# Linear attention and gated FFN on one core: reordering the first four units' state, mask, output and evacuation work

## The chip, the cores and the metric

One core of a Trainium2 chip. The metric is the device time of one execution in microseconds (us); lower is better.

## The reference, cut to what matters

```python
# q, k, v: [4, 8, 768, 64]; lam: [8]; blocks of 64 positions
for b in range(nb):
    intra = einsum('bhic,bhjc->bhij', qb, kb) * Dmask
    intra = einsum('bhij,bhjd->bhid', intra, vb)
    inter = einsum('bhid,bhde->bhie', qb * lam_pow, kv_state)
    out[:, :, sl] = intra + inter
    kv_state = lam_block * kv_state + einsum('bhsd,bhse->bhde', kb * rev_pow, vb)
x = out.transpose(0, 2, 1, 3).reshape(3072, 512)
return (x @ w_a) * (x @ w_b) @ w_out
```

Decayed linear attention, then a bilinear FFN on its 3072 rows.

## The kernel before

The kernel cuts the rows into 24 units of 128. Attention of a group of units is woven between the FFN products of the group before it. The first group, units 0 to 3, has nothing to hide behind: its attention runs first, and the FFN starts when its output `xT` is copied out of PSUM. The change edits only that start. For each unit *intra* multiplies masked scores with v, *inter* multiplies q with the state of the units before, and both add up in one PSUM tile `o`.

```python
def mask(kq, split=False):
    ...
        if split and i == 1:           # one mask of eight goes by ScalarE to GpSimd
            nc.scalar.copy(raw_kq, kq[i])
            nc.gpsimd.tensor_mul(m, raw_kq, lotri_bc)
        else:
            nc.vector.tensor_mul(m, kq[i], lotri_bc)

def inter(u):      # 4 products, full array: lhsT = state [128 x 128]
def intra(u):      # 8 products, lhsT = vb [128 x 64]: half the array's columns each

def kv_copy(u, ps, eng="dve"):         # state out of PSUM
    if eng == "act":                   # two copies of 64 x 256
    else:                              # one product of 128 x 512 with bdiag
    ...
def evac_o(u, xT, col, eng="act"):     # o[128 x 512] -> xT, by ScalarE or VectorE
    ...
    for u in range(n0):                # n0 = 4
        make_vb(u, "pool")             # v cast to bf16 on GpSimd
    ...
    scores4(1, (0, 1), ((5, 2), (6, 0)))
    for hps in ((0, 1), (2, 3)):
        for u in range(3):
            kv_part(u, hps)            # kv products: 2 * (u + 1) each time
            if hps[0]:
                kv_copy(u, sts[u], ("act", "act", "dve")[u])
    ...
    intra(0, True)
    evac_o(0, *xTs[0])
    intra(1, True)
    inter(1)
    evac_o(1, *xTs[1], eng="dve")
    intra(2, True)
    intra(3, True)
    inter(2)
    evac_o(2, *xTs[2], eng="dve")
    inter(3)
    evac_o(3, *xTs[3])
```

(`...` marks cuts. Unit 0 has no state before it, so no inter.)

## Time and profile before

| | before |
|---|---|
| median, first three runs | 233.85 us (233.6 to 234.01) |
| span of the profiled run, its time | 231.8 us, 233.49 us |
| TensorE busy | 97% of the span |
| first FFN product starts | 18.59 us |
| TensorE's last wait of note | 0.45 us, just before that product |

Read it this way: after 18.59 us TensorE waits for next to nothing, so the time is that start plus a constant. The lines are in the prediction.

### The profile page before, as it was taken

Reading aid. Unit: us, or ns where it says so; the run is one execution under the profiler, and the core shown is the slowest. Engines: PE = TensorE matmul, PEld = TensorE weight load, DVE = VectorE, ACT = ScalarE, POOL = GpSimd, SP = SyncE. Lnnn points to the kernel's source line nnn. Section 1 sums busy time; section 2 is a strip of 40 time slices with the busy share of each in tenths; the row PEclk is TensorE's granted clock in tenths of the full one; section 3 lists DMA queues with packets and bytes.
Section 4 is the critical chain, followed back from the end, with each engine's and each line's share of the span. In section 5 each row is a group of like instructions: output and inputs, shape, how many; then the busy total and the mean of one; then the engine's idle time right before and its main releaser. Section 6 shows DMA issues by size and latency. Waiting matters only on the chain.

```text
span 231.8 us, 4520 instructions
## 1 busy us (share of the span) xinstructions
PE 225.2 (97%) x1775; PEld 124.6 (54%) x1775; DVE 115.9 (50%) x204; ACT 91.1 (39%) x172; POOL 50.6 (22%) x65
## 2 busy tenths in 40 slices
PE   7799999999999999999999999999999999999994
PEld 2474444449698554454544454544454544444494
DVE  0896566636469726684334484235583323332050
ACT  3585754066463342333233332333332233332251
POOL 6070000248373333445000543001200000000000
PEclk9999999999999999999999999999999999999999
DMA  4999999999999999998759997229300220000311
GB/s 151 303 283 351 348 364 293 295 207 223 185 225 176 224 208 209 209 197 190 270 189 200 220 182 121 91 96 205 65 3 0 91 93 0 1 0 5 130 49 48
DMA packets 96389, 38.84 MB, mean 168 GB/s; under 512 B 83312, under 2 KB 91888, under 8 KB 96368
## 3 DMA queue, kind: packets, MB, share of 16 engines
q1 hardware_dynamic: 96224, 38.54, 72.9%
q8 instruction: 14, 0.23, 0.4%
q14 instruction: 7, 0.06, 0.1%
q10 hardware_dynamic: 144, 0.00, 0.0%
HBM read 28.32 MB, written 6.29 MB: 149 GB/s over the span
## 4 chain that ended last, share of the span: by engine, by line
PE 92%; DMA 3%; ACT 2%; SPq 1%; DVE 0%; issue 0%
PE a_ps L435 27%; PE b_ps L435 27%; PE op L467 27%; DMA k<-in_k_dram 3%; PE o_ps L352 3%; PE kq L310 2%; PE o_ps L342 2%; PE kvd L366 2%; PE tps L296 1%; ACT o_kept L458 1%; SPq L209 1%; PE kq L578 1%; ACT xT L359 0%; PE kv L366 0%; PE tk L542 0%; DVE scratch L531 0%
## 5 line engine op out<-in xcount | busy, mean ns | idle before, releaser
L447 DVE TENSOR_TENSOR ab<-a_sb,b_ps 128x512 bf16<-128x512 bf16 (+2 forms) x96 | 52.3, 552 | 77.9 <-PE b_ps L435 56.9
L435 PE MATMUL a_ps<-xT,wa_sb 128*128 128x512 bf16 (+2 forms) x384 | 77.2, 326 | 0.6 <-ACT xT L359 0.6
L435 PE MATMUL b_ps<-xT,wb_sb 128*128 128x512 bf16 (+2 forms) x384 | 77.2, 326 | 0.0
L442 ACT CAST a_sb<-a_ps 128x512 bf16<-128x512 f32 (+2 forms) x96 | 45.6, 481 | 63.1 <-PE a_ps L435 61.5
L467 PE MATMUL op<-wo_sb,ab 128*128 128x512 bf16 (+2 forms) x312 | 65.6, 363 | 0.0
L435 PEld LDWEIGHTS <-wb_sb 128*128 128x128 bf16 x384 | 34.5, 98 | 28.7
L435 PEld LDWEIGHTS <-wa_sb 128*128 128x128 bf16 x384 | 33.7, 98 | 29.1 <-POOL wa_sb L162 0.6
L467 PEld LDWEIGHTS <-ab 128*128 128x128 bf16 x312 | 28.8, 98 | 29.9
L327 DVE TENSOR_TENSOR m<-kq,lotri 128x512 bf16<-128x512 f32 x47 | 29.3, 682 | 18.1 <-PE kq L310 17.8
L259 POOL TENSOR_TENSOR qk<-kf,lp_k 128x512 bf16<-128x512 f32 x18 | 18.9, 1049 | 74.7 <-DMA kf<-in_k_dram 47.3
L264 POOL TENSOR_TENSOR qk<-qf,lp_q 128x512 bf16<-128x512 f32 x20 | 22.0, 1099 | 23.4 <-DMA qf<-in_q_dram 23.4
L462 ACT COPY o_sb<-op 128x512 f32<-128x512 f32 (+2 forms) x19 | 10.3, 541 | 34.0 <-PE op L467 34.0
L359 ACT CAST xT<-o_ps 128x512 bf16<-128x512 f32 x22 | 12.0, 590 | 17.9 <-PE o_ps L352 17.5
L398 DVE TENSOR_TENSOR st<-kvd,bdiag 128x512 bf16<-128x512 f32 x18 | 12.3, 682 | 4.9 <-PE kvd L366 3.8
L273 DVE CAST vb<-vf 128x512 bf16<-128x512 f32 x17 | 9.4, 553 | 0.0
L298 ACT COPY qkT<-tps 128x1024 bf16<-128x1024 bf16 x5 | 5.1, 1012 | 9.9 <-PE tps L296 9.9
L197 PE MATMUL idle<-idle_sb 128*128 128x128 bf16 (+1 forms) x31 | 7.2, 372 | 1.3 <-DVE idle_sb L192 1.3
L352 PE MATMUL o_ps<-m,vb 128*64 128x128 bf16 x192 | 7.9, 222 | 0.0
L273 POOL CAST vb<-vf 128x512 bf16<-128x512 f32 x7 | 4.7, 666 | 14.0 <-DMA vf<-in_v_dram 14.0
L342 PEld LDWEIGHTS <-st 128*128 128x128 bf16 x80 | 5.4, 98 | 2.8
L310 PE MATMUL kq<-qkT 64*128 64x128 bf16 x160 | 6.6, 218 | 0.0
L352 PEld LDWEIGHTS <-vb 128*64 128x64 bf16 x192 | 5.8, 109 | 1.4
(57 smaller groups left out, 87.4 us busy)
## 6 DMA issues: line engine op xcount, KB each, us to landing
vf<-in_v_dram SPq DMA_DIRECT2D x24, 256.0 KB, 4.9
qf<-in_q_dram SPq DMA_DIRECT2D x20, 256.0 KB, 4.4
kf<-in_k_dram SPq DMA_DIRECT2D x20, 256.0 KB, 4.6
out_dram<-o_sb SPq DMA_DIRECT2D x16, 256.0 KB, 2.0
wst<-in_moe_w_a_dram SPq DMA_DIRECT2D x6, 512.0 KB, 8.7
wst<-in_moe_w_b_dram SPq DMA_DIRECT2D x6, 512.0 KB, 8.8
wst<-in_moe_w_out_dram SPq DMA_DIRECT2D x6, 512.0 KB, 8.5
out_dram<-o_kept SPq DMA_DIRECT2D x7, 256.0 KB, 2.5
```

The costliest lines, as they stand in the source:

```text
L259: eng_of(eng).tensor_mul(qk[:, 1], raw.pop((u, "k")), lp_k[:, u % NB].to_broadcast([128, H, D]))
L264: eng_of(eng).tensor_mul(U[u]["qk"][:, 0], raw.pop((u, "q")), lp_q[:, u % NB].to_broadcast([128, H, D]))
L273: eng_of(eng).tensor_copy(vb, vf)
L310: nc.tensor.matmul(kq[i][:, hp, :], lhsT=d["kT"][p, hp, :], rhs=d["qT"][p, hp, :], start=True, stop=True, skip_group_check=True)
L327: nc.vector.tensor_mul(m, kq[i], lotri_bc)
L352: nc.tensor.matmul(d["o"][p, hp, :], lhsT=d["vb"][:, 2 * hp + i, :], rhs=d["m"](i, hp), start=(first and hp == 0), stop=True, skip_group_c ...
L359: nc.scalar.copy(xT[:, :, col:col + BLK], o_ps)
L398: nc.vector.tensor_mul(st[:].rearrange("p hp i d -> p hp (i d)"), ps[:].rearrange("p hp i d -> p hp (i d)"), bdiag_bc)
L435: nc.tensor.matmul(ps[:, :gt], lhsT=w_sb[:, s, f * 128:(f + 1) * 128], rhs=xT[:, s, :gt], start=(s == 0), stop=(s == KS - 1))
L442: nc.scalar.copy(a_sb[:, :gt], ps[:, :gt])
L447: nc.vector.tensor_mul(ab[:, f, :gt], a_sb[:, :gt], ps[:, :gt])
L467: nc.tensor.matmul(op[:, lo:hi], lhsT=ab[:, f, t * 128:(t + 1) * 128], rhs=wo_sb[:, f, lo:hi], start=(f == 0), stop=(f == FC - 1))
```

## The change

The intent: unit 0's and 1's states complete sooner, so that ScalarE is free sooner; GpSimd's mask no longer waits behind a v cast; ScalarE takes unit 2's evacuation while TensorE computes unit 3; and unit 3's, the last and exposed one, is shared by two engines. The whole diff:

```diff
-    for u in range(n0):
+    for u in range(n0 - 1):
         make_vb(u, "pool")
     ...
     scores4(1, (0, 1), ((5, 2), (6, 0)))
-    for hps in ((0, 1), (2, 3)):
-        for u in range(3):
-            kv_part(u, hps)
-            if hps[0]:
-                kv_copy(u, sts[u], ("act", "act", "dve")[u])
+    make_vb(3, "pool")
+    for u in range(2):
+        kv_part(u, (0, 1))
+    for u in range(2):
+        kv_part(u, (2, 3))
+        kv_copy(u, sts[u], "act")
+    kv_part(2, range(HP))
+    kv_copy(2, sts[2], "dve")
     ...
     intra(2, True)
+    inter(2)
+    evac_o(2, *xTs[2])
     intra(3, True)
-    inter(2)
-    evac_o(2, *xTs[2], eng="dve")
     inter(3)
-    evac_o(3, *xTs[3])
+    xT, col = xTs[3]
+    o3 = U[3].pop("o")
+    nc.scalar.copy(xT[:, 0:2, col:col + BLK], o3[:, 0:2])
+    nc.vector.tensor_copy(xT[:, 2:4, col:col + BLK], o3[:, 2:4])
```

## The prediction

> **What bounds the kernel now.** I read the page first, then the waits of TensorE, then the timeline of each engine from 14 to 19.5 us, where the edited lines run.
>
> From the page: the engines' busy time and the chain that ended last.
>
> ```profile
> PE 225.2 (97%) x1775; PEld 124.6 (54%) x1775; DVE 115.9 (50%) x204; ACT 91.1 (39%) x172; POOL 50.6 (22%) x65
> PE 92%; DMA 3%; ACT 2%; SPq 1%; DVE 0%; issue 0%
> ```
>
> TensorE is busy for 97% of the 231.8 us and is 92% of the chain. The next view lists all that TensorE ever waited for (total us, times, longest).
>
> ```profile
> PE idle L197 <- DVE idle_sb L192: 1.3, 1, 1.3
> PE tq L542 <- DVE scratch L531: 0.8, 4, 0.2
> PE tk L542 <- DVE scratch L531: 0.7, 2, 0.4
> PE a_ps L435 <- ACT xT L359: 0.6, 2, 0.5
> PE tn L562 <- ACT scratch L553: 0.2, 1, 0.2
> ```
>
> Only one of these is near the change: the first FFN product (L435) waits 0.45 us for the last evacuation of xT (L359). The remaining 0.1 us of that row is the only TensorE wait after it. So from the first FFN product on, TensorE runs its own stream with nothing to wait for, and the time of the kernel is the start of that product plus a constant. The whole question is: at what time does the first FFN product start, and can the three behind it follow it? In the kernel before it starts at 18.59 us. TensorE there:
>
> ```profile
> 14.19 0.67 PE L366 MATMUL kv<-vb,scratch 128*128 128x128 bf16 x6
> ...
> 15.36 0.50 PE L366 MATMUL kvd<-vb,scratch 128*128 128x128 bf16 x6
> 15.79 0.64 PE L352 MATMUL o_ps<-m,vb 128*64 128x128 bf16 x16
> 16.36 0.40 PE L342 MATMUL o_ps<-scratch,st 128*128 128x128 bf16 x4
> 16.69 0.68 PE L352 MATMUL o_ps<-m,vb 128*64 128x128 bf16 x16
> 17.30 0.62 PE L342 MATMUL o_ps<-scratch,st 128*128 128x128 bf16 x8
> 17.75 0.39 PE L562 MATMUL tn<-ident,scratch 128*128 128x128 bf16 x4
> 18.59 1.24 PE L435 MATMUL a_ps<-xT,wa_sb 128*128 128x512 bf16 x5 [0.45 <-ACT xT L359]
> ```
>
> L366 are the kv products, L352 intra, L342 inter. One row follows the other with no idle time marked. A product here lasts 0.22 us but the next is issued 0.056 us later (six products in 0.50 us: 0.22 + 5 x 0.056). So TensorE, not ScalarE, paces this stretch until 17.92 (17.30 + 0.62), the end of the last inter product. The other engines:
>
> ```profile
> 15.40 1.51 ACT L396 CAST st<-kv 64x256 bf16<-64x256 f32 x4 [0.50 <-PE kv L366]
> 16.94 0.59 ACT L359 CAST xT<-o_ps 128x512 bf16<-128x512 f32 x1
> 17.95 0.59 ACT L359 CAST xT<-o_ps 128x512 bf16<-128x512 f32 x1 [0.43 <-PE o_ps L342]
> 15.66 1.16 POOL L325 TENSOR_TENSOR m<-scratch,lotri 128x512 bf16<-128x512 bf16 x1
> 17.73 0.69 DVE L361 CAST xT<-o_ps 128x512 bf16<-128x512 f32 x1 [0.25 <-PE o_ps L342]
> ```
>
> ScalarE idled 0.43 us before unit 3's evacuation, waiting for TensorE. So the tail of the stage is: last inter product ends 17.92, +0.04, ScalarE copies for 0.59 to 18.54, +0.05, first FFN product at 18.59. GpSimd's mask ends at 16.82 (15.66 + 1.16), 0.13 after intra of unit 2 began at 16.69; that intra reads the mask in its sixth product, which by the 0.056 rhythm would have come at 16.83, and came at about 16.87. So the mask cost TensorE about 0.04 us.
>
> **What the Trainium skill says.** TensorEngine Tiling (Array Packing), section Key Properties: changing the tiling mode, not just the tile, drains TensorE. This trace agrees: intra is in mode 128*64, kv and inter in 128*128. The last of the 16 intra products is issued 0.22 before 16.43, at 16.21, and the next inter product at 16.36: 0.15 us. From inter to the transposes of L562, the same mode, it is 17.70 to 17.75, 0.056. A switch thus costs about 0.095 us more than going on.
>
> PSUM — Partial Sum Buffer, section PSUM bank collisions raise a hardware error: two engines may not access one bank in the same partitions at the same time, ScalarE and VectorE reading it included, and must be guarded by semaphores per bank and quadrant. No trace here shows a collision, but the built program shows the guard: in the changed kernel's order, VectorE's half copy of unit 3 waits for ScalarE's semaphore alone, at the count that ScalarE's half copy of the same bank reaches. So the two halves run one after the other, not side by side.
>
> **The change part by part.** I replay the stage with the rhythms above.
>
> 1. kv products of units 0 and 1 first. The 24 products stay 24, in one mode; they end at 15.86 as before. Unit 0's state is complete after 8 products rather than 14: six steps of 0.056 = 0.34 us earlier. ScalarE's four copies of L396 (1.51 us) move from 15.40–16.91 to about 15.06–16.57; it is free of its cast (L324) at 14.90, so nothing is in the way. Evacuation of unit 0 ends about 17.19 instead of 17.52. TensorE waited for none of them: inter of unit 1 came at 16.36, exactly one switch after intra, with its state ready at 16.14. Worth on the path: 0.
>
> 2. The mask ahead of unit 3's v cast. ScalarE's cast of the raw scores ends at 14.90, so GpSimd runs the mask at about 14.95–16.10 and the v cast (0.62) to 16.7. Both are there when wanted (16.69, and 17.36 for unit 3's intra). Removes the 0.04 us of TensorE's wait.
>
> 3. New order intra 2, inter 2, intra 3, inter 3, in place of intra 2, intra 3, inter 2, inter 3. This lets ScalarE evacuate unit 2 while unit 3 is computed, but adds two mode switches: 2 x 0.095 = 0.19 us, plus the first pair of products after a switch, which is 0.02 slower than a pair in stride. Replay: intra 2 16.69 to its last issue at 16.88; inter 2 issued 17.03–17.21, done 17.43; intra 3 17.36–17.55; inter 3 17.70–17.88, done 18.10. Before: 17.92. So the last inter product comes 0.18 us later. Evacuation of unit 2 on ScalarE runs 17.47–18.06, so ScalarE is just free for unit 3 at 18.14.
>
> 4. Unit 3 in halves. ScalarE's half, 128x256: its copies of 256 columns (L396) take 0.37 in place of 0.59, so it ends at 18.14 + 0.37 = 18.51. VectorE's half starts after that. Its duration is an estimate: VectorE's product L447 takes 686 ns at 512 columns and 416 at 256 by the groups by form, 0.27 less, so 691 - 270 = 420 ns; about 18.55–18.97.
>
> Start of the FFN: products read xT in four parts; parts 0 and 1 are ScalarE's half, 2 and 3 VectorE's. First product at 18.51 + 0.05 = 18.56 (before 18.59). Products follow each other at 0.215 us, so the third wants VectorE's half at 18.99 and gets it at 18.97 + 0.05 = 19.02; before it ran at 18.59 + 0.43 = 19.02. Sum: +0.18 (order) - 0.22 (shorter last copy) = -0.04 for the first product, and +0.03 of new wait in front of the third: about 0.00 us in all.
>
> After that: VectorE's cast of the first wb chunk slips from 18.34–19.02 to about 18.9–19.6; it is wanted at 20.1 or later. The next chunk's cast waits for its DMA till 20.79 in any case. Neither reaches the path.
>
> **The rivals.**
>
> A. The intent holds: unit 3's evacuation really halves, because VectorE and ScalarE are both free. For it: VectorE's last evacuation ends at 18.42 before. If the halves ran side by side, xT would be whole at 18.56 and the gain 0.03 us; the two extra drains eat the rest. If moreover the drains cost nothing, the last inter ends at 17.88 (0.04 for the mask), the first FFN product starts at 18.34, and the time falls by 0.25 us, to 233.6. Against it: the semaphore above, and 0.15 us at every switch in the stretch (15.64 to 15.79, 16.21 to 16.36, 17.15 to 17.30).
>
> B. The serial halves cost more than I say: VectorE starts late or takes 0.5 us or more. Then the third FFN product waits until 19.2 or so, and the kernel is 0.1 to 0.2 us slower, 234.0. For it: ScalarE-then-VectorE adds a semaphore hop; against it: two FFN products of 0.215 us lie over VectorE's half.
>
> C. Starting TensorE's FFN earlier runs into weights. The second chunks arrive by DMA: VectorE's cast of wa waited for it till 20.79 and ended 21.48, its first product came at 22.27, so there is 0.8 us of slack. A gain as small as A's would not be eaten. It matters only if the gain were larger than I can construct.
>
> **Range and chances.** Point: 233.85 + 0.00, 233.8. All three ways lie within 0.25 us, about 0.1%, which is less than the spread of the three runs before (233.6 to 234.01). The range is therefore mostly run to run noise, widened a little for another chip and for A and B: 233.3 to 234.3. For 2% something would have to move by 4.7 us, and the whole edited stretch is 4.5 us long. Faster by over 2%: 0.005; within 2%: 0.99; slower by over 2%: 0.005.
>
> **What would show each step right or wrong.** Step 1: ScalarE's L396 copies start near 15.06. Step 2: the mask ends near 16.1 and intra 2 shows no gap. Step 3: four separate rows of o_ps after 16.69, 0.15 us at each switch, last inter ending near 18.10; an end near 17.9 would refute the drains. Step 4: VectorE's 128x256 copy starts after ScalarE's ends, near 18.55; an overlap would refute the serial halves. Sum: the first FFN product at 18.5 to 18.6 with a wait named for ScalarE, and a small one for VectorE before the third. I would be wrong if the FFN starts before 18.4 or after 18.8, or if the span from there to the end (213.2 us) changes by more than the runs scatter, which would mean that something later depends on this stage.

## The result, and the profile after

The changed kernel: 233.57 us median of 5 runs (233.44 to 234.43); before, 233.85 us of 5 (233.6 to 234.01). The ratio of the fast runs is 0.9995, 95% interval 0.9975 to 1.0015: no difference that time alone can show. The results of every experiment are recorded as correct. The kernel runs on one core, and the granted clock was 0.993 to 1.0 throughout.

TensorE's timeline of the changed kernel answers to the one in the prediction (start us, us, engine, line, operation; what ended idle time in brackets):

```profile
15.78 0.64 PE L352 MATMUL o_ps<-m,vb 128*64 128x128 bf16 x16
16.35 0.40 PE L342 MATMUL o_ps<-scratch,st 128*128 128x128 bf16 x4
16.68 0.41 PE L352 MATMUL o_ps<-m,vb 128*64 128x128 bf16 x8
17.02 0.40 PE L342 MATMUL o_ps<-scratch,st 128*128 128x128 bf16 x4
17.35 0.41 PE L352 MATMUL o_ps<-m,vb 128*64 128x128 bf16 x8
17.70 0.40 PE L342 MATMUL o_ps<-scratch,st 128*128 128x128 bf16 x4
...
18.55 1.70 PE L435 MATMUL a_ps<-xT,wa_sb 128*128 128x512 bf16 x6 [0.24 <-ACT xT L640]
```

Rows alternate between intra (128*64) and inter (128*128), and the last inter product ends at 17.70 + 0.40 = 18.10; before it was 17.92. The first FFN product starts at 18.55; before 18.59. So 0.18 us went into the longer product sequence, and 0.22 came back from the shorter last copy. The step from the last intra product to the first inter product takes 0.15 us whether inter adds to the tile that intra has just written (16.87 to 17.02 here) or to another (17.15 to 17.30 before), so it is not a wait for that sum. (One of the first eight FFN products, the second, has no record in this trace; a trace can lack some. The third product is at 19.01, before it was at 19.02.)

The other engines, of the changed kernel:

```profile
14.97 1.16 POOL L325 TENSOR_TENSOR m<-scratch,lotri 128x512 bf16<-128x512 bf16 x1 [0.41 <-ACT scratch L324]
...
15.05 1.51 ACT L396 CAST st<-kv 64x256 bf16<-64x256 f32 x4 [0.17 <-PE kv L366]
...
16.07 0.61 POOL L273 CAST vb<-vf 128x512 bf16<-128x512 f32 x1
...
17.45 0.58 ACT L359 CAST xT<-o_ps 128x512 bf16<-128x512 f32 x1 [0.28 <-PE o_ps L342]
...
18.13 0.37 ACT L640 CAST xT<-o_ps 128x256 bf16<-128x256 f32 x1
...
18.53 0.42 DVE L641 CAST xT<-o_ps 128x256 bf16<-128x256 f32 x1 [1.06 <-ACT xT L640]
```

State copies start 0.35 us earlier; the mask ends at 16.13; and VectorE, idle for 1.06 us, is released by ScalarE's half copy (L640), not by TensorE. The halves run one after the other.

One thing in this profile was not in the prediction. What TensorE waited for in this run:

```profile
PE op L467 <- issue: 0.5, 3, 0.2
PE a_ps L435 <- ACT xT L640: 0.2, 1, 0.2
PE kvd L366 <- DVE st L398: 0.2, 1, 0.2
```

The last row, and a smaller stop later, are new. (The first row appears in the five traces that lack product records, this one among them, and costs nothing: the weight loads there go on in step.) By the starts of the same weight loads in both traces, TensorE in this run lost 0.32 us at 74 us and 0.21 us at 81 us, 55 us and more after the edited stretch; and the run ended 0.4 us later after its last product. This profiled run was the slowest of the five (234.43). Experiments 1 and 7 ask whether the change caused that.

### The profile page after: what moved, and what is told of

Read it like the earlier page. It is cut to its first block, busy times and chain, and to the rows that moved or that the text cites. A ratio compares the mean times of both kernels' runs of the same rounds, so it can differ in the third digit from the quotient of the medians.

```text
span 232.7 us, 4499 instructions
## 1 busy us (share of the span) xinstructions
PE 223.8 (96%) x1752; PEld 124.7 (54%) x1775; DVE 118.0 (51%) x204; ACT 91.4 (39%) x173; POOL 50.7 (22%) x65
## 3 DMA queue, kind: packets, MB, share of 16 engines
q1 hardware_dynamic: 96224, 38.54, 72.8%
## 4 chain that ended last, share of the span: by engine, by line
PE 82%; DMA 7%; SPq 4%; DVE 1%; issue 1%; POOL 1%; ACT 1%; POOLq 0%; DVEq 0%
PE a_ps L435 25%; PE b_ps L435 25%; PE op L467 21%; DMA k<-in_k_dram 3%; PE o_ps L352 3%; SPq L128 3%; PE kq L310 2%; DMA qf<-in_q_dram 2%; PE o_ps L342 2%; DMA kf<-in_k_dram 2%; PE kvd L366 1%; POOL qk L259 1%; SPq L144 1%; PE tps L296 1%; SPq L209 1%
## 5 line engine op out<-in xcount | busy, mean ns | idle before, releaser
L467 PE MATMUL op<-wo_sb,ab 128*128 128x512 bf16 (+2 forms) x300 | 64.1, 362 | 0.9 <-issue 0.5
L327 DVE TENSOR_TENSOR m<-kq,lotri 128x512 bf16<-128x512 f32 x47 | 29.3, 683 | 17.6 <-PE kq L310 17.3
L259 POOL TENSOR_TENSOR qk<-kf,lp_k 128x512 bf16<-128x512 f32 x18 | 18.8, 1042 | 75.3 <-DMA kf<-in_k_dram 68.6
L398 DVE TENSOR_TENSOR st<-kvd,bdiag 128x512 bf16<-128x512 f32 x18 | 12.3, 682 | 4.6 <-PE kvd L366 3.8
L273 DVE CAST vb<-vf 128x512 bf16<-128x512 f32 x17 | 11.8, 691 | 0.0
```

The costliest lines, as they stand in the source:

```text
L259: eng_of(eng).tensor_mul(qk[:, 1], raw.pop((u, "k")), lp_k[:, u % NB].to_broadcast([128, H, D]))
L273: eng_of(eng).tensor_copy(vb, vf)
L398: nc.vector.tensor_mul(st[:].rearrange("p hp i d -> p hp (i d)"), ps[:].rearrange("p hp i d -> p hp (i d)"), bdiag_bc)
L467: nc.tensor.matmul(op[:, lo:hi], lhsT=ab[:, f, t * 128:(t + 1) * 128], rhs=wo_sb[:, f, lo:hi], start=(f == 0), stop=(f == FC - 1))
```

## The experiments

Stage times repeat to about 0.03 us between runs while total times scatter by 0.5 us and more, so I judge the parts of the change by the start of the FFN in the profile, and use total times only where several rounds were run. "Shift" is how far a run's whole stretch is displaced before the edited part takes effect: the start of the first intra product against the same product of the kernel it was edited from. The other runs are single executions; of those only the profile is used.

**1. The changed kernel again** (no edit).

> The changed kernel once more, to tell what is fixed from what scatters. My theory: the edited stretch is the same to 0.02 us (first FFN product at 18.55, third at 19.01), while the waits of TensorE near 74 and 81 us (0.3 and 0.2 us in the first profile, none before the change) are scatter of that one run: they are absent, or of another size. Time 233.5 to 233.9, ratio 1.000 within 0.002. Rival: the change itself causes these two waits by moving GpSimd against VectorE; then they are there again, at the same places and sizes, and the time is 0.3 us or more above the kernel before.

Measured: 233.57 us median of 6 (233.43 to 236.23), ratio 1.0014 (0.9979 to 1.005). First FFN product 18.58, third 19.04, with a shift of 0.03. At 74 us TensorE lost 0.06 us in this profile, and at 81 nothing. So the stops of the first profile are not fixed to the change. One of the six runs, 236.23 us, lifts the ratio above 1. It was not profiled; its granted clock of 0.993 is that of the run with a late first load in experiment 6, which suggests the same cause but does not show it.

**2. Part 3 alone: the new product order.**

```diff
     intra(2, True)
-    intra(3, True)
     inter(2)
     evac_o(2, *xTs[2], eng="dve")
+    intra(3, True)
     inter(3)
     evac_o(3, *xTs[3])
```

> The kernel before with nothing but the new order intra 2, inter 2, intra 3, inter 3 (engines of the copies as before). Drain theory: two more mode switches, so the last inter product ends 0.18 to 0.23 us later than 17.92, near 18.14, and the first FFN product starts near 18.8. Rival, switches cost nothing and only the late copies held TensorE: last inter still ends near 17.92 and the first FFN product starts at 18.59 or before.

```profile
16.66 0.41 PE L352 MATMUL o_ps<-m,vb 128*64 128x128 bf16 x8
17.01 0.40 PE L342 MATMUL o_ps<-scratch,st 128*128 128x128 bf16 x4
17.34 0.41 PE L352 MATMUL o_ps<-m,vb 128*64 128x128 bf16 x8
17.68 0.40 PE L342 MATMUL o_ps<-scratch,st 128*128 128x128 bf16 x4
...
18.75 1.02 PE L435 MATMUL a_ps<-xT,wa_sb 128*128 128x512 bf16 x4 [0.45 <-ACT xT L359]
```

The same instructions in another order end 0.16 us later (18.08), and the FFN starts 0.16 us later (18.75). I expected 18.14 and 18.8; in this run the mask ended at 16.75, early enough to cost TensorE nothing. From the start of unit 2's intra to the end of the last inter product it is 1.42 us with the new order (here and in the changed kernel) and 1.19 us with the old order and an early mask (experiments 3 and 6): two switches cost 0.23 us. The rival, free switches, falls.

**3. Part 2 alone: the mask first.**

```diff
-    for u in range(n0):
+    for u in range(n0 - 1):
         make_vb(u, "pool")
     ...
     scores4(1, (0, 1), ((5, 2), (6, 0)))
+    make_vb(3, "pool")
```

> The kernel before with only GpSimd's mask moved ahead of unit 3's v cast. If my step 2 is right: the mask ends near 16.1, the 0.04 us gap in intra of unit 2 goes, last inter ends near 17.88 and the first FFN product starts near 18.55, so 0.04 us early. Rival: unit 3's v cast, now the later one (end 16.7), holds intra 3, and nothing or less is gained.

Mask end 16.14, last inter 17.87, first FFN product 18.55: as expected, 0.04 us. Yet its single time was 234.29: TensorE lost 0.9 us at 74 and 81 us (see 7).

**4. Part 1 alone: kv products of units 0 and 1 first.**

```diff
-    for hps in ((0, 1), (2, 3)):
-        for u in range(3):
-            kv_part(u, hps)
-            if hps[0]: ...
+    for u in range(2): kv_part(u, (0, 1))
+    for u in range(2):
+        kv_part(u, (2, 3)); kv_copy(u, sts[u], "act")
+    kv_part(2, range(HP)); kv_copy(2, sts[2], "dve")
```

> The kernel before with only the kv products of units 0 and 1 first. My step 1: ScalarE's four state copies start near 15.06 rather than 15.40 and the evacuation of unit 0 ends near 17.2, but the first FFN product stays at 18.59 (0.00). Rival: earlier states let inter of unit 1 or 2 start earlier and the FFN starts before 18.5.

State copies from 15.10 (shift 0.04), evacuation of unit 0 ends at 17.23, first FFN product 18.59: the work moved 0.3 us and the path 0.00.

**5. Are the halves serial because of the shared bank?** The changed kernel, unit 3's output in two banks.

```diff
-    o3 = U[3].pop("o")                       # one tile, one bank
+    o3 = [ps_bank("o_ps", [128, 2, 128], F32, at=at) for at in (6, 0)]
+    ...                                      # the same 12 products into o3[hp // 2]
-    nc.scalar.copy(xT[:, 0:2, col:col + BLK], o3[:, 0:2])
-    nc.vector.tensor_copy(xT[:, 2:4, col:col + BLK], o3[:, 2:4])
+    nc.scalar.copy(xT[:, 0:2, col:col + BLK], o3[0])
+    nc.vector.tensor_copy(xT[:, 2:4, col:col + BLK], o3[1])
```

> The changed kernel, but unit 3's output lies in two banks, one for each half, so that the halves may be copied side by side. If the shared bank is what puts VectorE's half after ScalarE's: now they overlap, both starting within 0.1 us of 18.13, VectorE's ends near 18.55, and the third FFN product runs at 18.98 rather than 19.02, with no wait for VectorE; the first stays at 18.55. Gain 0.03 us, because two FFN products hide the second half anyway. Rival: the order comes from the copies' destination (both write xT), then VectorE's half still starts near 18.53.

```profile
18.05 0.37 ACT L646 CAST xT<-o_ps 128x256 bf16<-128x256 f32 x1
...
18.16 0.42 DVE L647 CAST xT<-o_ps 128x256 bf16<-128x256 f32 x1 [0.65 <-PE o_ps L644]
```

They overlap, and VectorE now waits for TensorE. The destination is the same tile as before, so it is the shared source that put them in line. The edit gives each half its own PSUM tile along with its own bank, so it does not tell a shared bank from a shared PSUM tile; that two engines read one tile is not enough by itself, for VectorE (L327) and GpSimd (L325) read `lotri`, a tile in SBUF, at the same time in every trace. The first FFN product started at 18.47 and the third ran at 18.90, which is 0.11 us before the changed kernel's third in spite of a shift of +0.03, and more than the 0.03 I expected: ScalarE's half started at 18.05, before the last inter product ended at 18.13, because it no longer waits for the two inter products that write the other half.

**6. All but part 3: the old order, halves.** The changed kernel with intra 2, intra 3, inter 2, inter 3, and unit 2 on VectorE.

```diff
     intra(2, True)
+    intra(3, True)
     inter(2)
-    evac_o(2, *xTs[2])
-    intra(3, True)
+    evac_o(2, *xTs[2], eng="dve")
     inter(3)
     ...                                      # the halves, as in the changed kernel
```

> The changed kernel with the old product order (intra 2, intra 3, inter 2, inter 3) and unit 2 again copied by VectorE; unit 3 in halves. Drain theory: last inter ends near 17.88, ScalarE's half near 18.28, VectorE's copy of unit 2 near 18.38, so the first FFN product starts near 18.42, 0.13 us before that of the changed kernel, and the third near 18.85. Rival: the new order was what the change lived on, and the first FFN product comes at 18.55 or later.

This run took 235.89 us, because lam, one of its first loads, came late. The row of the kernel before and then of this run:

```profile
4.34 0.21 ACT L220 ACTIVATE loglam<-lam_sb 128x8 f32<-128x8 f32 x1 [1.81 <-DMA lam_sb<-in_lam_dram]
```

```profile
6.58 0.21 ACT L220 ACTIVATE loglam<-lam_sb 128x8 f32<-128x8 f32 x1 [4.05 <-DMA lam_sb<-in_lam_dram]
```

A load of 4 KB that landed 2.2 us late moved everything behind it by 2.3 us. So the same kernel ran again:

> The same kernel as in old_order_halves, whose only run began 2.3 us late because the small load of lam came late. Taking that 2.3 us off, its first FFN product stood at 18.52 and the wait was for VectorE's copy of unit 2. If that reading is right: without a late lam the first FFN product is at 18.52 to 18.55, VectorE's copy of unit 2 ends near 18.38, and the time is 233.5 to 234.0 instead of 235.89. Rival: the 2.3 us belong to the kernel and come again.

```profile
17.23 0.62 PE L342 MATMUL o_ps<-scratch,st 128*128 128x128 bf16 x8
...
18.50 1.24 PE L435 MATMUL a_ps<-xT,wa_sb 128*128 128x512 bf16 x5 [0.43 <-DVE xT L361]
```

Last inter at 17.85 and VectorE's copy of unit 2 at 18.36, as predicted; the first FFN product at 18.50, 0.05 us before the changed kernel, not 0.13. My step from the copy's end to the product, 0.05 us, was too short here: it took 0.15. In the first of these two runs the path is to be seen: copy ends 20.67, a semaphore instruction of TensorE's queue runs 20.71 to 20.76, the weight load starts at 20.79, the product at 20.82. In these traces a wait that sits in front of the weight load is dearer than one on the product itself (0.15 against 0.05 us). The kernel before had the same wait: VectorE's copy of unit 2 ended at 18.42, and 0.15 us later is 18.57, only 0.02 us before the FFN started there. So halving ScalarE's last copy alone, with unit 2 left on VectorE, could gain little: that copy was next in line. The third product ran at 18.93, 0.08 us before the changed kernel's. So with unit 2 left to VectorE, the change is slightly better without its part 3.

**7. Where the scatter comes from: the late v casts on ScalarE.** The changed kernel, one word edited.

```diff
-        make_vb(u, "pool" if u < n0 + 3 else "dve")
+        make_vb(u, "pool" if u < n0 + 3 else "act")
```

> The changed kernel with the v casts of units 7 and on moved from VectorE to ScalarE, to test where the scatter comes from. Theory: VectorE's v cast is held while GpSimd works on its scalings (0.42 us alone, 0.7 to 0.9 where they meet near 73 and 80 us), which delays the state and then TensorE at 74 and 81 us. Then without these casts on VectorE TensorE's losses at 74 and 81 us go, and the times scatter less (within 0.3 us). Rival: the losses come from late DMA alone; they stay or move to ScalarE, whose cast now stands in the queue before FFN evacuations, and the time rises by 0.3 us or more.

First, how the theory arose. Around 72.8 us, the kernel before and then the changed one in its first profile:

```profile
71.90 1.04 POOL L264 TENSOR_TENSOR qk<-qf,lp_q 128x512 bf16<-128x512 f32 x1
...
72.85 0.41 DVE L273 CAST vb<-vf 128x512 bf16<-128x512 f32 x1
...
73.51 0.68 DVE L398 TENSOR_TENSOR st<-kvd,bdiag 128x512 bf16<-128x512 f32 x1
```

```profile
72.25 1.04 POOL L264 TENSOR_TENSOR qk<-qf,lp_q 128x512 bf16<-128x512 f32 x1
...
72.84 0.74 DVE L273 CAST vb<-vf 128x512 bf16<-128x512 f32 x1
...
73.83 0.68 DVE L398 TENSOR_TENSOR st<-kvd,bdiag 128x512 bf16<-128x512 f32 x1
...
74.56 0.38 PE L366 MATMUL kvd<-vb,qk 128*128 128x128 bf16 x4 [0.19 <-DVE st L398]
```

VectorE's cast starts at the same time in both. GpSimd's scaling ends at 72.94 in the first and 73.29 in the second, and the cast ends 0.3 us after it in both (73.26, 73.58). The state (L398) and TensorE's kv product follow. In the run of experiment 3 GpSimd ended at 73.63, the cast took 1.11 us and ended at 73.92, and TensorE waited 0.56 us. The Trainium skill, SBUF — State Buffer, section SBUF: two separate sides, says that VectorE's two-port modes and GpSimd share one port pair as an exclusive lock that the loser waits for; the three numbers agree with that, though no trace here shows in which mode the cast runs. The profile shows a longer cast, not a wait.

Measured with the casts on ScalarE: TensorE's losses at 74 and 81 us are gone from the profile, with 0.1 us at 70 us in their place; times 233.62 to 233.81 in five runs and 234.28 in one; ratio to before 1.0002 (0.9982 to 1.0021). GpSimd's work was not early by chance in this profile: the first of its two scalings near 72 us began at 71.24, as late as in the changed kernel's first profile (71.25), where 0.32 us was lost. So the mechanism is supported by the profile. That it makes the times scatter less is not shown by six runs, and 234.28 breaks the 0.3 us that I expected. And it gains nothing: the profile of the kernel before lost nothing there either.

TensorE's losses between 70 and 82 us, relative to the profile of before: 0.54 (changed kernel), 0.06 (again), 0.13 (order only), 0.89 (mask first), 0.14 (kv first), 0.01 (two banks), 0.20 and 0.01 (old order, first and second run), 0.08 (experiment 7), 0.77 (experiment 8), 0.01 (experiment 9), 0.08 (experiment 10). They go with no part of the change. The time from TensorE's last product to the end of the span scatters too, from 3.00 to 3.56 us in the thirteen profiles (3.10 before); why is open. What sets GpSimd's start in a given run I did not settle; in the profile of before it was released by the landing of k (L259, 70.89 us).

**8. If switches are what costs: group the products by mode.** The changed kernel with intra 0, 1, 2, then inter 1, 2, 3, then intra 3: three switches from the kv products to the last product on the outputs, in place of six. Inter 3 now opens unit 3's accumulation.

```diff
     intra(1, True)
+    intra(2, True)
     inter(1)
     evac_o(1, *xTs[1], eng="dve")
-    intra(2, True)
     inter(2)
     evac_o(2, *xTs[2])
-    intra(3, True)
-    inter(3)
+    ...                                      # inter 3, start=(hp == 0)
+    intra(3)
```

> The changed kernel with the products grouped by mode: intra 0, 1, 2, then inter 1, 2, 3, then intra 3: three switches in place of six. Drain theory: last product on the outputs ends near 17.77 (18.09 in the changed kernel), ScalarE's half near 18.18, first FFN product near 18.23 and third near 18.67: 0.32 us before the changed kernel and 0.36 before the first kernel, to 233.2 in runs without late waits, ratio to the kernel before 0.9985. Rival: another wait (a state, the v cast, the weights' cast) takes its place and the FFN starts at 18.45 or later; or the gain is given back later in waits for the weights.

First FFN product 18.26, third 18.72, with a shift of 0.03: 0.29 us before the changed kernel. No weights were waited for. Times: 233.52 us median of 6 (233.23 to 234.03), ratio to before 0.9992 (0.9974 to 1.001). The profiled run lost 0.77 us near 74 us and so gave no gain in time. Right in the stage, unresolved in the time.

**9. The same with two banks.** The edit of 8, and unit 3's output in two banks as in 5.

> three_switches with unit 3's halves in two banks. ScalarE is busy with unit 2 till 17.85, so its half stays near 17.85 to 18.22 and the first FFN product near 18.26; VectorE's half moves beside it (17.8 to 18.25) and the third product comes at 18.69 rather than 18.72. Time as three_switches within noise: 233.2 to 233.6 where no late wait falls in, ratio to the kernel before 0.9985 (0.997 to 1.000). Rival: ScalarE's half starts earlier as in two_banks and the first FFN product comes near 18.15.

```profile
15.86 0.86 PE L352 MATMUL o_ps<-m,vb 128*64 128x128 bf16 x24
16.66 0.62 PE L342 MATMUL o_ps<-scratch,st 128*128 128x128 bf16 x8
17.11 0.39 PE L640 MATMUL o_ps<-scratch,st 128*128 128x128 bf16 x4
17.43 0.41 PE L644 MATMUL o_ps<-m,vb 128*64 128x128 bf16 x8
...
18.22 1.46 PE L435 MATMUL a_ps<-xT,wa_sb 128*128 128x512 bf16 x6
```

Three long rows in place of six short ones: the last product on the outputs ends at 17.84 in spite of a shift of 0.08, and the FFN starts at 18.22, third product at 18.65. Time: 233.34 us median of 4 (233.04 to 233.6); before, 233.62 of 12; ratio 0.9979 (0.9965 to 0.9994). Of the six comparisons with several runs this is the only one whose interval lies below 1, and it rests on four runs. The 0.37 us by which the FFN starts earlier would be 0.16%, which lies within the interval; the medians differ by 0.28 us. In its profile, which lost nothing at 74 and 81 us, the last product ended 0.36 us earlier than before, but what follows that product took 3.56 us in place of 3.10. It was not run against the changed kernel in the same rounds; of that one the ratio to before was 0.9995 and 1.0014.

**10. The same with the late v casts on ScalarE as well** (the edits of 7 and 9).

> grouped_two_banks with the late v casts on ScalarE as well. If VectorE's cast held by GpSimd is what costs 0.1 to 0.8 us near 74 and 81 us, this one starts its FFN at 18.26 and loses nothing there, only the 0.1 us near 70 that casts_on_act showed: 233.3 median, every run within 0.3 us of it except late first loads; ratio to the kernel before 0.9980 to 0.9990, interval below 1. Rival: the gain of the early FFN start is lost anyway to waits for loads, and the median is 233.6 like the others.

233.45 us median of 4 (233.38 to 233.51), ratio 0.9988 (0.9975 to 1.0001); FFN from 18.21, third product 18.64, 0.11 us lost near 70, none at 74 or 81. The times lie closer together than those of any other version, but four runs are few, and the interval touches 1.

## Why the prediction was right

Step by step, in its own order.

- The bound: that TensorE's stream after the first FFN product is a constant. Held within 0.1 us in six of the twelve later profiles, but too strong for each of them. "Nothing to wait for" was read off one profile; other runs lost up to 0.9 us near 74 and 81 us. By the prediction's own sign of being wrong, a stretch from the first FFN product to the end that changes by more than the scatter, the first profile would have refuted it (214.2 us in place of 213.2); only the second (213.5) showed that this is not fixed to the change. This is the statement of the prediction that the runs corrected: I had covered it as run to run noise without knowing its source.
- Step 1, kv products first, worth 0 on the path. State copies at 15.05 (said 15.06); alone, the FFN stayed at 18.59. Right.
- Step 2, the mask, 0.04 us. Mask end 16.13 (said 16.10); alone, the FFN moved from 18.59 to 18.55. Right.
- Step 3, two more switches. Last inter at 18.10 (said 18.10); the order alone delayed the FFN by 0.16 us. Right.
- Step 4, halves in line: VectorE's half 18.53 to 18.96 (said 18.55 to 18.97), serial; experiment 5 shows that sharing one bank (and one PSUM tile) is the cause. Right. The estimate of 0.42 us for VectorE's copy was met.
- The sum: first product 18.55 (said 18.56), third 19.01 (said 19.02). The change takes 0.22 us from the last copy and gives 0.18 to mode switches, and what is left of the gain in front of the first product is used up by the third's wait for the second half.
- The time, 233.57 us for a point of 233.8, lies inside a range that is mostly noise, so it confirms little: the stage times above do. Two costs were mis-sized without consequence for the sum. A wait in front of the weight load takes 0.15 us and not 0.05, and the prediction did not see that in the kernel before VectorE's copy of unit 2 held the FFN back almost as long as ScalarE's of unit 3 (18.57 and 18.59). It was luck that this did no harm: part 3 takes that copy off VectorE.
- Rival A did not come about, for both of the reasons given, but its 0.03 us for halves side by side was too small: experiment 5 gained 0.11 us at the third product. B neither, since the copy was not longer than estimated; C was tested by experiment 9, where the FFN began 0.37 us earlier and still waited for no weights.

So the gain that the change was made for, a shorter last evacuation, went into the product order that was meant to feed it.

## What to carry to other kernels

When a change shortens the last step of a chain, recount what it adds to the step before: here a reorder that let a copy start early put two array-mode switches in front of it, and grouping the products by mode was worth more than the whole change (the FFN started 0.33 us before that of the first kernel in experiment 8, and 0.04 us before it in the changed one). If two engines are to share the copy of one result, give each half its own PSUM bank. And when the stage edited is 2% of the kernel, judge by a stage time in the profile that repeats to a few hundredths of a microsecond, not by totals that scatter ten times as much.

## What the Trainium skill lacked or had wrong

- TensorEngine Tiling (Array Packing), Key Properties, says that a mode switch drains TensorE but not what it costs: 0.15 us from issue to issue instead of 0.056 between full-array and half-column products here, and 0.23 us for two extra switches in experiment 2.
- PSUM — Partial Sum Buffer, PSUM bank collisions raise a hardware error, agrees with the order seen here; it gives no figure for what it costs a kernel to split one bank's copy over two engines: VectorE's half started 0.40 us after ScalarE's in one bank (18.13 and 18.53) and 0.11 us after it in two (18.05 and 18.16).
- SBUF — State Buffer, SBUF: two separate sides, agrees on the lock, but not how the profile shows it: VectorE's cast of 0.41 us appears as one of 0.74 or 1.11 us with no wait, ending 0.3 us after GpSimd's instruction (experiment 7).
- No page that I read gives the cost of a wait in front of a weight load against one on the product: 0.15 us against 0.05 us from the copy's end to the product's start (experiment 6).
- No page that I read warns that one small first load can set the start of everything: lam, 4 KB, landed 2.2 us late in one run and cost 2.3 us.
